# A new order for the 1215 pieces of an attention and feed-forward kernel

## The chip, the cores and the metric

One core of a Trainium2 chip. The metric is the device time of one execution in microseconds (us), lower is better. All engines of the core are used: TensorE (PE) for matmuls, with its weight loads shown apart as PEld, VectorE (DVE), ScalarE (ACT), GpSimd (POOL), SyncE (SP, which only issues DMAs), and the 16 DMA engines.

## The reference

Attention over 4 batches, 8 heads, 768 positions, head size 64, and then a two-layer feed-forward with 512 inputs and 2048 hidden units:

```python
scores = scale * np.matmul(q, k.transpose(0, 1, 3, 2))
stream_keep = causal & (is_sink | in_win)        # 4 sink positions, window of 64
mask = np.where(retr[0, :, 0, 0, None, None], causal, stream_keep)
a = softmax(np.where(mask, scores, -1e9))
x = np.matmul(a, v)                              # heads side by side: 3072 x 512
h = x @ w_in
g = np.maximum(h, 0.0) + alpha * np.minimum(h, 0.0)
out = g @ w_out
```

Heads 0, 2 and 6 are full causal ("retrieval") heads; the other five see only the first 4 positions and the last 64.

## The kernel before

The work is cut into 1215 named pieces. Each piece is a small function that emits a few instructions; `item(name, fn, ...)` stores it, and a list of names, `ORDER`, says in which order all pieces are emitted. The program is scheduled by hand: each engine runs its own instructions in the order in which they were emitted, and waits on semaphores only where a piece needs the result of another engine or a buffer that another engine still uses. So the list is at once the queue of every engine. A piece that waits holds up everything that stands behind it on the same engine, and nothing on the others.

The attention is done in 16 segments n, one for each batch and pair of heads (pairs (2,6), (1,5), (0,4), (3,7)); segments 0 to 3 are the first batch. The names of their pieces:

- `Lq`, `Lk`, `Lv` load rows of q, k and v (lines 234 to 282). They go on SP's queue, q1 in the profile's list of DMA queues.
- `Cq`, `Ck`, `Cv` cast the rows to bf16, on the engine that the strings CQ, CK and CV name for that segment: POOL for segments 1 to 5 (CQ, CK) and 0 to 5 (CV), VectorE for most later ones (lines 351 to 391).
- `Tq`, `Tk` transpose on TensorE (line 406), `tq`, `tk` copy the result out of PSUM (lines 411 to 437). From segment 8 on, `Dq` and `Dk` do this by a transposing DMA on SP.
- `S` computes scores (lines 456 to 473 and 505, 544), `s` exponentiates them on ScalarE (lines 512, 560 to 566), `m` masks them on VectorE (lines 522, 571, 574).
- `A` multiplies with v (line 595), `a` divides by the row sum (lines 605, 606), `X` transposes the result into `xT` (by TensorE, line 620, for segments 0 to 3 and 15, else by DMA on SP, line 614), `x` copies it.

The feed-forward goes by 8 blocks t of tokens, 512 and 256 tokens of each batch in turn:

- `P t.f` multiplies with `w_in` for a group of hidden units (line 640). For some blocks it is cut into parts by input chunk: `P0.f.0` needs segments 0 and 1, `P0.f.1` segment 2, `P0.f.2` segment 3.
- `p` takes the negative part by a relu on ScalarE (line 645), `g` makes the activation on VectorE (line 652).
- Block 0 has its output in pieces `O` (line 660) and `o` (copy, and store on POOL's queue). The other blocks use seven products instead of eight for each 256 x 256 piece (a Strassen-like scheme): `D` are combinations of `w_out`, `Z` those of g (lines 684, 703, VectorE), `Q` the products (line 718), `b1` to `b8` the copies and additions that end in the store (lines 742 to 771).

The weights are loaded on POOL's queue (q0), by a DMA that casts from fp32 to bf16, and so stand in one line with POOL's casts and masks: `wi0a`, `wi0b`, `wi1a`, `wi1b` are half loads for the first 512 hidden units (line 819; the a halves hold the input chunks of segments 0 and 1, the b halves those of 2 and 3), `wi2` to `wi7` the other columns of `w_in` (line 824; 2 and 3 for f 4 to 7, 4 and 5 for f 8 to 11, 6 and 7 for f 12 to 15), `wo0` to `wo3` the rows of `w_out` (line 828). `nr` (line 786) and `ns` (lines 792 to 804) make masks on POOL for the later segments; `kfz` are memsets on POOL. `warm` pieces are matmuls on a buffer of zeros with no reader (line 814).

PSUM has eight banks. `take` gives a piece the bank that was freed longest ago among those that it may use, at the time of emission; so the order also decides which bank a piece waits for.

Scores of segments from 4 on aren't emitted where they stand: `one_score` collects them in `burst`, and `emit_burst` sends the collection when a piece comes that is not in the set of `beside_burst`. Where both heads of a pair have 576 columns or more in the burst, or where the pair is of one kind from segment 8 on, the two heads are sent in turn on the upper and the lower half of the array (64 rows each, line 473), so that they run side by side; else they go one after the other (line 466). So the order also decides how many bursts there are and how they run.

Of the kernel before, what the change touches and what calls it, by code (L numbers as in the profile page):

```python
# [34 lines left out]
A5.0 s7.1.2 O0.3.1 Cv6 m4.1.5 S6.0.2 Cv7 m4.1.3 s7.1.1 Dq8 s6.0.1 O0.3.2 m6.0.4 o0.2 a5.0 m6.0.5 S7.0.0 s7.1.0 Dk9.0
s7.0.2 A6.1 O0.3.3 m6.0.1 S7.0.1 Cq9 m7.1.0 s6.0.2 m6.0.0 s7.0.0 A4.1 m7.0.0 S8.0.0 S8.1.0 s7.0.1 S8.0.5 m6.0.3 S8.1.3
m7.1.1 S8.0.3 a6.1 S8.1.1 m7.1.2 o0.3 s8.0.3 A6.0 X5 a4.1 s8.0.5 A7.1 Q1.0.1 m7.0.2 s8.1.3 s8.1.0 m7.0.1 m6.0.2 s8.1.1
A7.0 a7.1 b1.1.0 Dq9 S9.1.1 a6.0 a7.0 S8.0.2 Lq10 S8.1.4 S8.0.1 X4 Q1.0.2 S9.1.0 S9.0.1 s8.0.0 Z1.0.2 D3.1 S9.0.2
s8.0.1 Z1.0.4 s8.0.2 m8.1.1 S8.1.2 X6 s8.1.4 s9.0.1 Q1.0.5 s8.1.2 Q1.0.6 s9.1.0 s9.0.2 s9.1.1 S8.1.5 D4.0 S8.0.4
S9.0.0 b2.1.0 S9.1.2 X7 s8.1.5 P2.2.0 m8.0.5 P2.11.0 s8.0.4 P2.5.0 m9.1.0 s9.0.0 m8.1.3 m8.0.0 m9.1.1 P2.5.1 Cq10 D3.0  # L40
b3.1.0 P2.2.1 kfz2 s9.1.2 p2.5 m10.0.2 Lk10 m8.0.3 Lv9 p2.2 P2.3.0 P2.3.1 g2.2 nz0 b7.1.0 Q1.0.7 P2.11.1 m9.0.1 g2.5
p2.11 m8.0.4 g2.11 p2.3 P2.1.0 P2.13.0 m8.1.4 b4.1.0 P2.8.0 P2.6.0 P2.1.1 Q1.0.3 P2.8.1 Dq10 m9.1.2 m9.0.2 P2.13.1
m9.0.0 Lq11 P2.7.0 g2.3 p2.1 P2.6.1 p2.13 P2.7.1 Cv9 p2.6 m8.0.1 b8.1.0 P2.9.0 b5.1.0 g2.1 Cq11 g2.6 P2.0.0 P2.15.0
p2.7 g2.7 Ck10 m8.1.0 P2.0.1 p2.8 g2.8 p2.0 P2.14.0 Lv8 A9.0 Lk11 g2.0 Dq11 g2.13 P2.14.1 P2.15.1 P2.4.0 p2.15 P2.4.1
a9.0 p2.14 A9.1 Cv8 Dk10.1 Q1.0.4 g2.14 P2.9.1 b6.1.0 p2.4 P3.0 a9.1 P2.12.0 P2.12.1 P3.4 g2.15 p3.0 A8.0 p2.12
P2.10.0 Dk10.0 P2.10.1 Ck11 S10.1.0 g2.4 Lv11 g2.12 Dk11.0 p2.9 g2.9 Q2.1.1 p2.10 g3.0 b1.2.1 S10.0.1 s10.1.0 p3.4
S10.0.4 s10.0.1 g2.10 Z2.1.1 Q2.0.1 X9 Lv10 b1.2.0 Q2.1.2 S10.0.0 s10.0.0 Z2.0.1 g3.4 Lk14 s10.0.4 S10.0.3 s10.0.3
Z2.1.3 Lk12 a8.0 Q2.0.2 P3.12 b7.2.0 S10.0.5 Lq15 Z2.1.2 b7.2.1 S10.1.2 m10.0.0 S11.0.1 p3.12 S11.1.1 Lq12 Z2.0.3
m14.0.2 m12.0.2 S10.1.1 S11.0.2 Q2.1.6 s11.1.1 s10.1.2 s11.0.2 g3.12 m8.1.5 s10.0.5 b2.2.1 m11.0.2 Z2.0.2 P3.6 s11.0.1
P3.2 b3.2.1 S10.0.2 S11.0.0 S11.1.2 S11.1.0 s10.1.1 s11.0.0 m10.1.2 Q2.1.5 Lv14 A8.1 s10.0.2 m10.1.0 s11.1.0 Q2.1.7  # L50
m10.0.4 m10.0.5 P3.14 m11.1.1 Z2.1.4 p3.6 Cv11 b4.2.1 Q2.0.6 Cv10 m10.1.1 s11.1.2 Q2.1.3 A10.1 g3.6 b5.2.1 Q2.1.4
m10.0.1 m10.0.3 P3.10 b2.2.0 b3.2.0 a8.1 b8.2.1 a10.1 A10.0 kfz3 m11.0.0 m11.1.2 m11.0.1 A11.0 a10.0 p3.2 Q2.0.5
b6.2.1 Lq13 m11.1.0 a11.0 P3.8 A11.1 Q2.0.7 p3.14 X8 Z2.0.4 p3.8 X10 b4.2.0 g3.2 Lk13 Q2.0.3 a11.1 p3.10 Q3.0.1 b8.2.0
b5.2.0 g3.14 P4.12.0 X11 P4.6.0 Lv12 Cq12 P4.1.0 g3.10 g3.8 P4.2.0 Q2.0.4 b1.3.0 P4.5.0 Cq13 P4.12.1 Ck12 P4.6.1 Lv13
P4.15.0 P4.15.1 Z3.0.1 Z3.0.3 P4.1.1 P4.5.1 Lq14 Z3.0.2 p4.12 P4.2.1 g4.12 Dq12 Q3.0.2 p4.2 b7.3.0 Ck13 p4.1 P4.13.0
Ck14 b6.2.0 g4.2 p4.15 Q3.0.6 g4.1 p4.6 p4.5 P4.13.1 g4.15 p4.13 P4.4.0 b2.3.0 Q3.0.5 Dq13 b4.3.0 Z3.0.4 P4.10.0
Dk12.0 P4.8.0 g4.6 P4.14.0 P4.8.1 P4.10.1 b3.3.0 P4.4.1 g4.5 Cv13 Q3.0.7 P4.14.1 P5.2 Q3.0.3 p4.8 g4.8 p4.10 p4.4
b5.3.0 g4.13 g4.4 Lv15 p5.2 P4.3.0 Cv12 p4.14 Cq14 g4.10 P4.3.1 P5.12 S12.0.0 S12.1.2 Cq15 g5.2 p4.3 Dk13.0 Q3.0.4
b8.3.0 g4.14 P5.8 s12.0.0 S12.1.4 p5.12 s12.1.2 S12.0.2 b6.3.0 S12.0.5 S13.1.0 Lk15 P5.6 Dq14 s12.0.5 p5.8 g5.12 p5.6
P4.0.0 P4.11.0 Dk14.1 s12.0.2 g4.3 m12.0.0 Dk14.0 s12.1.4 Cv15 P4.0.1 P4.11.1 s13.1.0 m12.0.5 g5.6 p4.11 P4.7.0 Dq15  # L60
g5.8 P4.7.1 S12.0.1 p4.0 S13.1.2 S12.1.5 g4.11 S13.0.0 P4.9.0 g4.0 s12.0.1 p4.7 P4.9.1 s13.0.0 g4.7 P5.10 P5.4 p4.9
S12.1.0 m12.1.4 S12.1.3 g4.9 S13.0.1 s12.1.5 p5.10 Z4.0.1 S12.0.3 s13.1.2 p5.4 Ck15 s12.1.3 Q4.0.1 g5.4 s12.0.3 g5.10
m13.1.2 Q4.0.5 s13.0.1 s12.1.0 S12.0.4 S12.1.1 S14.1.2 b1.4.0 S13.1.1 m12.0.3 m12.1.3 S14.0.3 Z4.0.3 m12.0.1 S13.0.2
Z4.0.2 m13.1.0 s12.1.1 Q4.0.2 s12.0.4 b7.4.0 Z4.0.4 m12.0.4 s13.1.1 Dk15.0 Q4.1.1 b1.4.1 P5.14 Z4.1.1 A12.0 s13.0.2
s14.0.3 m12.1.5 S14.0.2 m13.1.1 Q4.0.6 m13.0.2 a12.0 S14.0.4 s14.0.2 p5.14 s14.1.2 Z4.1.3 Q4.1.2 b2.4.0 m13.0.0 A13.1
s14.0.4 m14.1.2 S14.0.1 b3.4.0 P5.0 a13.1 b4.4.0 p5.0 Q4.0.3 s14.0.1 Q4.0.7 g5.14 S15.1.2 g5.0 S14.1.1 S14.0.5 S15.0.0
m13.0.1 b5.4.0 m12.1.1 Z4.1.2 S14.0.0 b7.4.1 S15.1.1 m14.0.4 Q4.0.4 s15.1.2 Z4.1.4 s14.0.0 s14.1.1 s14.0.5 m14.0.0
m14.0.1 Cv14 m12.1.0 Q4.1.6 b6.4.0 s15.1.1 m14.0.5 A13.0 b2.4.1 m14.0.3 s15.0.0 S15.0.2 S15.1.0 S15.0.1 S14.1.0
s15.0.2 s14.1.0 m15.0.0 Q4.1.5 s15.1.0 m14.1.1 m14.1.0 A12.1 a13.0 A14.0 s15.0.1 m15.0.2 m15.1.1 a12.1 A14.1 a14.0
Q5.0.1 m15.1.0 a14.1 b3.4.1 b4.4.1 m15.0.1 Q4.1.7 m15.1.2 b1.5.0 X13 X12 b5.4.1 Q5.0.2 Q4.1.3 A15.0 Z5.0.1 X14 a15.0  # L70
A15.1 a15.1 Q4.1.4 b6.4.1 P6.8.0 X15 x15 P6.15.0 P6.4.0 b8.4.0 P6.8.1 P6.11.0 P6.10.0 b8.4.1 b7.5.0 P6.13.0 P6.4.1
P6.2.0 p6.4 P6.10.1 P6.11.1 P6.14.0 P6.2.1 P6.15.1 Z5.0.3 p6.8 p6.11 g6.4 P6.12.0 g6.8 P6.7.0 P6.12.1 P6.7.1 Z5.0.2
p6.15 g6.11 g6.15 P6.3.0 p6.2 g6.2 P6.13.1 p6.10 P6.9.0 P6.14.1 p6.13 P6.3.1 g6.13 p6.7 g6.10 p6.14 P6.1.0 P6.0.0
P6.9.1 g6.14 P6.5.0 p6.9 P6.1.1 p6.12 P6.6.0 g6.7 p6.3 g6.3 P6.6.1 P6.0.1 Q5.0.6 g6.9 P6.5.1 P7.6 p6.1 P7.4 g6.1
# [922 lines left out]
```

## Time and profile before

| | us |
|---|---|
| three runs | 222.61, 223.55, 223.62 (median 223.55) |
| span of the profiled execution, first to last instruction | 220.4 |
| whole time of the profiled execution | not listed apart |
| PE busy | 214.5 |
| DVE busy | 188.0 |
| ACT busy | 145.8 |
| POOL busy | 45.6 |

The median of the runs lies 3.15 us above the span of the profiled execution. In the profile, a "busy" matmul includes a modelled end, which lies behind the start of the next matmul; what TensorE loses is therefore seen better from the distance of the starts. In the rows of the stretches, the numbers are, for PE, PEld, DVE, ACT and POOL in turn, the busy us and in brackets the instructions; then the granted clock, the DMA engines' busy share (which adds up queues that overlap) and GB/s. In rows of the chain and of the timeline the first number is the start and the second the length, both in us.

### The profile page before, as it was taken

Reading aid. Unit: us, or ns where it says so; the run is one execution under the profiler, and the core shown is the slowest. Engines: PE = TensorE matmul, PEld = TensorE weight load, DVE = VectorE, ACT = ScalarE, POOL = GpSimd, SP = SyncE. Lnnn points to the kernel's source line nnn. Section 1 sums busy time; section 2 is a strip of 40 time slices with the busy share of each in tenths; the row PEclk is TensorE's granted clock in tenths of the full one; section 3 lists DMA queues with packets and bytes.
Section 4 is the critical chain, followed back from the end, with each engine's and each line's share of the span. In section 5 each row is a group of like instructions: output and inputs, shape, how many; then the busy total and the mean of one; then the engine's idle time right before and its main releaser. Section 6 shows DMA issues by size and latency. Waiting matters only on the chain.

```text
span 220.4 us, 5779 instructions
## 1 busy us (share of the span) xinstructions
PE 214.5 (97%) x2210; PEld 158.0 (72%) x2210; DVE 188.0 (85%) x471; ACT 145.8 (66%) x314; POOL 45.6 (21%) x92
## 2 busy tenths in 40 slices
...
DMA  6999999999999999979999998791004310002124
GB/s 187 319 233 222 307 241 231 227 201 218 205 245 167 259 162 222 198 182 193 211 215 174 228 184 194 176 187 42 4 1 123 103 79 0 0 3 95 51 93 147
DMA packets 89655, 35.98 MB, mean 163 GB/s; under 512 B 76676, under 2 KB 87964, under 8 KB 89628
## 3 DMA queue, kind: packets, MB, share of 16 engines
...
q10 hardware_dynamic: 320, 0.34, 0.5%
q14 instruction: 10, 0.08, 0.1%
HBM read 27.58 MB, written 6.29 MB: 154 GB/s over the span
## 4 chain that ended last, share of the span: by engine, by line
PE 92%; DVE 3%; ACT 2%; issue 1%
PE P L640 36%; PE P L718 28%; PE P L595 7%; PE P L660 7%; PE P L473 4%; PE P L814 3%; PE P L456 2%; PE P L406 2%; PE P L466 1%; PE P L620 1%; DVE kT L435 1%; PE P L544 1%; DVE g L652 1%; ACT neg L645 1%; ACT kT L435 0%
## 5 line engine op out<-in xcount | busy, mean ns | idle before, releaser
L640 PE MATMUL P<-xT,w_in_b 128*128 128x512 bf16 (+1 forms) x512 | 89.6, 326 | 0.0
L652 DVE SCALAR_TENSOR_TENSOR g<-neg,oma,P 128x256 bf16<-128x256 f32 (+1 forms) x128 | 71.7, 607 | 11.4 <-ACT neg L645 11.0
L645 ACT ACTIVATE neg<-P 128x512 f32<-128x512 f32 x96 | 55.4, 602 | 30.3 <-PE P L640 15.7
L640 PEld LDWEIGHTS <-w_in_b 128*128 128x128 bf16 x512 | 49.2, 98 | 29.1 <-issue 0.3
L718 PEld LDWEIGHTS <-g 128*128 128x128 bf16 x480 | 45.7, 98 | 8.1 <-issue 0.8
L512 ACT ACTIVATE eR<-P 128x448 bf16<-128x448 f32 (+4 forms) x63 | 37.0, 627 | 4.8 <-PE P L505 2.2
L718 PE MATMUL P<-w_out_b,g 128*128 128x256 bf16 x320 | 39.0, 273 | 0.0
...
L560 ACT ACTIVATE eS<-P 128x352 bf16<-128x352 f32 x45 | 20.8, 494 | 2.3 <-PE P L473 1.4
L606 DVE TENSOR_TENSOR xn<-P,rcp 128x448 bf16<-128x448 f32 (+1 forms) x32 | 19.4, 607 | 1.1
L571 DVE TENSOR_TENSOR eS<-eS,ms_near 128x352 bf16<-128x352 bf16 x45 | 15.8, 363 | 0.7 <-ACT eS L560 0.6
L660 PE MATMUL P<-w_out_b,g 128*128 128x512 bf16 x64 | 15.8, 379 | 0.2 <-ACT kT L429 0.2
L703 DVE TENSOR_TENSOR g<-g 128x1024 bf16<-128x1024 bf16 x20 | 13.7, 683 | 0.1
L456 PE MATMUL P<-qT,kT 128*128 128x192 bf16 (+14 forms) x68 | 11.1, 251 | 0.2 <-ACT eS L566 0.2
L595 PEld LDWEIGHTS <-eS 128*128 128x128 bf16 x260 | 10.0, 97 | 1.3
L595 PE MATMUL P<-vb,eS 128*128 128x65 bf16 x260 | 10.8, 193 | 0.0
L522 DVE TENSOR_TENSOR eR<-eR,mr_near 128x128 bf16<-128x128 bf16 (+5 forms) x54 | 10.6, 223 | 0.0
L473 PE MATMUL P<-qT,kT 64*128 64x176 bf16 (+10 forms) x164 | 10.4, 249 | 0.0
L718 PE MATMUL P<-w,g 128*128 128x256 bf16 x80 | 10.4, 273 | 0.0
L660 PEld LDWEIGHTS <-g 128*128 128x128 bf16 x64 | 5.6, 97 | 6.3 <-issue 1.1
L595 PE MATMUL P<-vb,eR 128*128 128x65 bf16 x276 | 10.0, 193 | 0.0
L595 PEld LDWEIGHTS <-eR 128*128 128x128 bf16 x276 | 9.4, 97 | 0.6 <-issue 0.2
(130 smaller groups left out, 267.8 us busy)
## 6 DMA issues: line engine op xcount, KB each, us to landing
out_dram<-ot POOLq DMA_DIRECT2D x18, 256.0 KB, 3.2
...
w_out_b<-in_moe_w_out_dram POOLq DMA_DIRECT2D x4, 512.0 KB, 15.1
...
```

The costliest lines, as they stand in the source:

```text
L456: nc.tensor.matmul(to, keys, queries, start=True, stop=stop)
L473: nc.tensor.matmul(to, keys[own], queries[own], start=True, stop=True)
L512: nc.scalar.activation(ebuf[n, hh][:, lo:hi].rearrange("p (x c) -> p x c", x=len(parts)), P[:, got[0]:got[0] + len(parts), 0:(hi - lo) // ...
L560: nc.scalar.activation(slots, sc[:, 0:352].rearrange("p (s c) -> p s c", c=176), AF.Exp, scale=scale)
L571: nc.vector.tensor_tensor(slots, slots, ms_near[:, 0:2, :] if m == 0 else ms_near[:, 1:3, :], op=ALU.mult)
L595: nc.tensor.matmul(pav[:, i, :], e[:, o:o + 128], vv[:, j, hh, 0:D + 1], start=(m == 0), stop=(m == len(terms) - 1))
L606: nc.vector.tensor_tensor(xn[n][:, 0:nt, D * hh:D * hh + D], pav[:, :, 0:D], rcp.to_broadcast([128, nt, D]), op=ALU.mult)
L640: nc.tensor.matmul(psg[:, w * i:w * (i + 1)], w_in_b[:, c, 128 * fb:128 * (fb + 1)], xT[:, c, o:o + w], start=(x == 0), stop=(x == 3))
L645: nc.scalar.activation(neg[t, f], bank(held["P", t, f][0]), AF.Relu, scale=-1.0)
L652: nc.vector.scalar_tensor_tensor(g_buf[t % 2][:, fb, 0:w], neg[t, f][:, c], oma[:, fb:fb + 1], bank(got[0])[:, c], op0=ALU.mult, op1=ALU.add)
L660: nc.tensor.matmul(bank(held["O", t, s][0]), g_buf[t % 2][:, f, 128 * s:128 * (s + 1)], w_out_b[:, f, :], start=(f == 0), stop=(f == 15))
L718: nc.tensor.matmul(q_bank(t, u, CHAIN[y]), left[t, u][y][:, f, :], right[y][:, f, :], start=(first and f == 0), stop=(f == 7), skip_group_ ...
```

## The change

Only `ORDER` changes. The first 40 names stay where they are, and the other 1175 stand in a new order over the whole rest of the list. No piece is added, removed or changed; each is emitted once. What follows from the list changes with it: the queue of each engine and of its DMAs, the PSUM bank that each piece gets, and the bursts of scores.

In POOL's queue, `wi0a`, `wi1a`, `wi1b`, `wi0b` stood together behind `Ck3.0` and now stand apart, with casts, `nr` and two `kfz` between them; `ns` now stands between `wi2` and `wi3`; `wo1` to `wo3` now stand behind `Cv4`. In SP's queue, `Lq3` now stands ahead of `Lv0`, `Lk4` ahead of `Lv3`, and `Lv4` ahead of `Lk7` and `Lq7`. In TensorE's queue the first pieces of blocks 0 and 1 come in another order, among them `P1.14` and `P0.15` ahead of `P0.13`. The core of the diff: the beginning of both lists, the part of the new one around Cv8, and the ends.

```diff
--- before.py
+++ after.py
 ORDER = """
-busy zero id warm0 kz3 Lq0.0 sz1 vz2 nms nmr so1 vz0 Lq0.1 Lk1 warm8 warm5 warm3 kz1 qz0 one Lq1 Lk0 La Ck0.0 kz2
-Cq0.0 Tq0.0 tq0.0 Tk0.0 qz warm2 Lk2 Lq2 kz0 tk0.0 Ck1.0 Ck1.1 Cq0.1 Tk1 S0.0.1 s0.0.1 Tq0.1 S0.0.0 Cq1 warm7 Lv0
-tk1.0 sz2 vz1 vz3 Tq1 Ck0.1 S0.0.2 s0.0.0 tk1.1 Tk0.1 Ck2.1 tq1 S1.1.0 s0.0.2 Ck2.0 warm4 tq0.1 s1.1.0 Cq2 tk0.1 Cv0
-Lk3 S0.1.0 kfz0 Lv1 vo ro0 Ck3.1 s0.1.0 Lq3 Ck3.0 wi1a wi0a wi1b wi0b Cq3 sz0 idf S1.0.0 so2 Al s1.0.0 so0 al S0.1.1
-s0.1.1 Lv2 Tq2 Tk2 tk2.1 tk2.0 S0.1.2 S1.0.1 A0.0 s0.1.2 a0.0 Cv1 A0.1 a0.1 Cv2 s1.0.1 tq2 S1.1.1 Tk3 S2.0.1 tk3.0
-s1.1.1 S2.0.2 X0 s2.0.1 x0 wi6 s2.0.2 wi7 Lv3 Lq4 Tq3 tk3.1 S2.0.0 wi5 m4.0.2 warm6 S2.1.0 A1.0 a1.0 Lk4 tq3 A1.1
-Cv3.0 s2.0.0 Lq5 Lk6 Lq6 Lk5 wi4 Cq4 a1.1 S3.0.0 s2.1.0 A2.0 s3.0.0 X1 x1 S3.0.1 S3.1.1 Ck4.0 P0.2.0 s3.0.1 A3.0 a2.0
-Lq7 a3.0 S2.1.1 s3.1.1 wi2 s2.1.1 Cv3.1 S3.1.0 wi3 A2.1 Ck4.1 Cq5 wo1 s3.1.0 P0.1.0 P0.3.0 A3.1 Lk7 P0.0.0 Tq4 a2.1
-tq4 X2 a3.1 X3 Lv5 Tk4 x2 P0.2.1 Lv6 P0.1.1 tk4.0 P0.3.1 P0.0.1 x3 Tq5 tq5 tk4.1 P0.0.2 P0.1.2 wo0 p0.0 P0.3.2 P0.13
-p0.13 g0.0 P0.14 g0.13 P1.14 wo3 p0.1 p1.14 g0.1 P1.2 p1.2 P0.8 Lv4 g1.14 Ck6.0 P0.9 g1.2 Cq6 m8.0.2 p0.8 nr p0.9 g0.8
-m12.1.2 p0.3 near0 near2 P0.15 S4.0.5 p0.14 P1.10 s4.0.5 Ck6.1 P0.11 P0.2.2 g0.9 Ck5.1 g0.14 p0.15 p1.10 P1.0 Lq8 Tq6
-ro1 Ck5.0 g0.15 p0.2 g0.3 S4.1.0 g1.10 wo2 p0.11 P1.12 P1.8 P0.7 g0.2 Lk8 s4.1.0 kfz1 g0.11 Lk9 p1.0 P0.5.0 p1.12 tq6
-g1.0 P0.5.1 Tk5 P0.4.0 p1.8 P0.6 tk5.0 g1.8 p0.7 P0.4.1 g1.12 P0.5.2 P0.4.2 p0.6 tk5.1 P0.10 g0.7 p0.4 p0.10 g0.6
-S4.0.3 s4.0.3 S4.0.0 P1.4 g0.4 Tk6 g0.10 S4.0.1 S5.1.0 m4.0.3 P1.6 p0.5 tk6.1 Ck7.0 near1 D1.0 P0.12 tk6.0 O0.0.0 g0.5
-O0.0.1 p1.6 Lv7 p0.12 g1.6 p1.4 S6.1.1 D1.1 s5.1.0 s4.0.0 S5.1.1 S4.1.2 g1.4 m4.1.0 s4.0.1 s4.1.2 Z1.0.1 s6.1.1 s5.1.1
-O0.1.0 S5.0.0 S4.0.4 S4.1.4 S4.1.1 g0.12 O0.1.1 s5.0.0 m4.0.5 s4.1.4 m4.0.0 Ck7.1 s4.1.1 ns S5.1.2 S4.0.2 S4.1.3
-S5.0.1 O0.0.2 s5.1.2 s4.1.3 D2.1 O0.0.3 O0.2.0 s5.0.1 m6.1.1 S6.0.4 s4.0.4 S5.0.2 S6.1.0 D4.1 m5.0.0 s4.0.2 Z1.0.3
-S6.0.0 m5.1.2 o0.0 S6.1.2 S4.1.5 Lq9 Cq7 Cv4 s5.0.2 m5.1.1 O0.1.2 D2.0 Tk7 s4.1.5 O0.2.1 Cv5 Tq7 m4.0.1 m5.0.2 s6.1.0
-m8.1.2 s6.1.2 O0.1.3 tk7.0 m5.1.0 m4.0.4 tk7.1 A4.0 Ck8 s6.0.0 tq7 A5.1 m4.1.2 S6.0.5 o0.1 m4.1.1 O0.2.2 Cq8 Dk8.0
...
-Q6.1.6 Z6.0.4 Q6.0.3 g7.12 b7.6.0 b8.6.0 b2.6.1 Q6.0.7 Z7.0.1 Z7.0.3 b3.6.1 b5.6.0 Q6.1.5 Q7.0.5 b4.6.1 Q6.0.4 Z6.1.4
-b1.7.0 Z7.0.2 Q7.0.2 Q6.1.7 Q7.0.6 Q6.1.3 b5.6.1 b4.7.0 b2.7.0 b7.6.1 b7.7.0 b6.6.0 b8.6.1 b3.7.0 Q6.1.4 Q7.0.7 b6.6.1
-Z7.0.4 Q7.0.3 b5.7.0 Q7.0.4 b8.7.0 b6.7.0
+busy zero id warm0 kz3 Lq0.0 sz1 vz2 nms nmr so1 vz0 Lq0.1 Lk1 warm8 warm5 warm3 kz1 qz0 one Lq1 Lk0 La Ck0.0 kz2 Cq0.0
+Tq0.0 tq0.0 Tk0.0 qz warm2 Lk2 Lq2 kz0 tk0.0 Ck1.0 Ck1.1 Cq0.1 Tk1 S0.0.1 S0.0.0 Lq3 s0.0.1 warm4 Cq1 s0.0.0 vz1 tk1.1
+Tq1 S0.0.2 Tq0.1 Ck0.1 tk1.0 Ck2.0 tq1 Cq2 Lv0 Lk3 Ck2.1 Cq3 s0.0.2 Tk0.1 warm6 tq0.1 S1.1.0 tk0.1 idf S1.0.0 s1.1.0
+warm7 S0.1.0 vz3 Cv0 sz2 Tq2 s1.0.0 S0.1.1 vo s0.1.0 Tk2 Al wi0a Ck3.0 S0.1.2 s0.1.1 s0.1.2 sz0 Ck3.1 al Lv1 so0 wi1a
+Lv2 A0.0 S1.0.1 tq2 s1.0.1 Cv1 nr tk2.1 ro0 A0.1 kfz3 S1.1.1 kfz1 Lk4 Tk3 tk2.0 ro1 Lv3 a0.1 a0.0 Cv2 tk3.0 s1.1.1
+S2.0.1 S2.0.0 s2.0.1 A1.0 a1.0 A1.1 Ck4.1 s2.0.0 S2.0.2 a1.1 Tq3 wi1b X0 s2.0.2 S2.1.0 tq3 wi6 tk3.1 X1 Ck4.0 S3.0.0 x0
+s2.1.0 Cv3.0 S3.0.1 A2.0 Lq4 Lq5 s3.0.0 s3.0.1 x1 S2.1.1 Cq4 s2.1.1 so2 S3.1.0 a2.0 A2.1 Cv3.1 Lq6 Tq4 S3.1.1 s3.1.0
+wi0b a2.1 A3.0 s3.1.1 Tk4 wi7 Cq5 P0.3.0 wi2 X2 tk4.0 ns Cq6 a3.0 wi3 wi4 A3.1 a3.1 tq4 P0.1.0 x2 P0.0.0 P0.2.0 wi5 Lk5
+Tq5 P0.3.1 P0.0.1 near0 P0.1.1 X3 Lk6 Tq6 P0.2.1 tq5 x3 P1.14 near2 S4.0.5 P0.2.2 Lv4 tq6 P0.0.2 P0.15 tk4.1 p0.2 P0.1.2
+s4.0.5 g0.2 P1.2 p0.0 P0.3.2 p1.14 g0.0 Lk7 Ck5.0 p1.2 g1.14 g1.2 p0.15 p0.1 g0.15 g0.1 Ck5.1 S4.1.4 P1.0 p0.3 wo0 P0.14
+Tk5 p0.14 S4.1.0 P1.4 g0.3 P0.13 Ck6.0 s4.1.0 Cv4 P0.9 p1.0 g0.14 p1.4 kfz0 tk5.1 g1.0 S4.0.3 Ck6.1 tk5.0 g1.4 P0.8 p0.9
+S5.1.2 P1.6 Lk8 s4.0.3 near1 g0.9 Lq8 P1.8 P0.5.0 p0.13 g0.13 p0.8 Lq9 P1.12 S4.0.0 s5.1.2 g0.8 D1.0 p1.6 P0.4.0 p1.8
+s4.1.4 m4.0.5 P0.11 s4.0.0 Tk6 P0.6 g1.6 p0.11 g1.8 P0.4.1 P0.5.1 p1.12 Ck7.0 p0.6 wo1 g0.11 S5.1.0 P0.7 wo2 g0.6 P0.5.2
+S5.1.1 g1.12 tk6.1 P0.4.2 P1.10 p0.7 s5.1.0 m5.1.2 s5.1.1 g0.7 p1.10 p0.5 Lv6 P0.12 Ck8 wo3 g0.5 tk6.0 p0.4 P0.10 m5.1.0
+S4.0.1 s4.0.1 O0.1.0 p0.12 O0.0.0 S5.0.0 g1.10 S5.0.2 g0.4 p0.10 g0.12 S6.1.2 S6.1.0 Lq7 O0.1.1 Lv5 O0.0.1 s6.1.2 s6.1.0
+Lk9 Z1.0.1 S6.1.1 s5.0.2 S4.1.3 S4.1.5 S4.0.4 g0.10 s5.0.0 S4.0.2 S5.0.1 s4.1.3 m4.0.1 Ck7.1 Cv5 D2.0 m4.0.0 m4.0.3
+O0.0.2 S6.0.4 s4.0.4 s4.0.2 m5.0.0 m5.0.2 s5.0.1 O0.0.3 S6.0.0 s6.1.1 S6.0.5 S4.1.2 s4.1.5 S4.1.1 m4.0.4 m4.1.5 Cq8
+s4.1.1 o0.0 O0.1.2 m5.0.1 m6.1.2 A4.0 s6.0.5 s6.0.0 Lv7 m5.1.1 s6.0.4 s4.1.2 m6.0.5 Tk7 m4.1.3 Cv6 kfz2 m6.1.0 m6.0.4
+O0.1.3 m6.1.1 S6.0.1 O0.2.0 O0.3.0 Cq7 S6.0.2 O0.2.1 Tq7 s6.0.1 O0.2.2 m6.0.1 tk7.0 Dk8.0 tq7 A5.0 o0.1 Ck9 a4.0 O0.2.3
+m4.1.0 s6.0.2 Z1.0.3 m4.1.1 S6.0.3 tk7.1 S7.0.1 Cq9 s7.0.1 m4.1.4 O0.3.1 a5.0 m7.0.1 D1.1 Dq8 o0.2 A5.1 s6.0.3 S7.0.2
...
+P2.12.1 g2.2 p2.15 P2.10.1 g2.1 Ck11 m8.0.1 g2.15 P2.4.1 P2.9.0 A9.1 Lq11 P2.13.0 Q1.0.4 Cq11 P2.0.1 p2.12 a9.1 Dk10.0
+p2.10 P2.13.1 g2.10 p2.4 g2.12 P2.9.1 p2.0 g2.4 P2.8.0 p2.9 S10.0.0 Lv8 P2.14.0 g2.0 P2.8.1 b6.1.0 Dq11 A9.0 Dk11.0
+p2.13 Dk10.1 Cv8 m8.1.4 p2.8 g2.13 a9.0 A8.0 g2.9 m8.0.2 P2.14.1 S10.0.4 P3.0 P3.4 Q2.0.1 a8.0 Lv10 g2.8 S10.0.1 S10.0.3
+s10.0.4 p2.14 S11.1.2 p3.0 s10.0.0 g3.0 S11.1.0 Lv11 Q2.1.1 p3.4 s10.0.1 P3.14 s11.1.0 s11.1.2 g2.14 b1.2.0 m8.1.0 g3.4
...
+g7.8 b1.6.1 Z6.1.2 Z6.0.2 p7.10 Q6.0.2 Q7.0.1 Q6.1.6 Q6.0.6 Z6.0.4 g7.10 b2.6.1 Z7.0.1 b2.6.0 b4.6.0 Q6.0.3 Q6.1.2
+b3.6.0 Q7.0.5 Z7.0.3 Q6.0.7 b3.6.1 Z7.0.2 b5.6.0 b7.6.0 Q7.0.6 b1.7.0 Q6.0.4 Z6.1.4 Q6.1.7 b4.6.1 b8.6.0 b2.7.0 Q7.0.2
+b3.7.0 b4.7.0 b6.6.0 b7.7.0 Q6.1.3 b5.6.1 b7.6.1 Q7.0.7 Q6.1.4 Z7.0.4 b5.7.0 Q7.0.4 b8.6.1 b6.6.1 b6.7.0 Q7.0.3 b8.7.0
 """.split()
```

81 lines of the change are left out of this document (37 added, 44 removed).

## The prediction

> **What bounds the kernel now.** I read the page first, then the busy time by stretches of 10 us, the waits of TensorE, the chain, and last the timeline of POOL with the landing of its loads.
>
> ```profile
> span 220.4 us, 5779 instructions
> PE 214.5 (97%) x2210; PEld 158.0 (72%) x2210; DVE 188.0 (85%) x471; ACT 145.8 (66%) x314; POOL 45.6 (21%) x92
> DMA  6999999999999999979999998791004310002124
> PE 92%; DVE 3%; ACT 2%; issue 1%
> ```
>
> TensorE holds 92% of the chain and is busy 97% of the span. The DMA row says something else as well: the 16 engines are full for the first 25 slices of 5.5 us. So TensorE sets the time, and for the first 130 us or so the loads leave little room.
>
> ```profile
> 0.00:10.00 10.00, 8.94 (x109) 8.31 (x110) 6.86 (x21) 5.99 (x7) 6.29 (x19) 1.00 0.81 253
> 10.00:20.00 10.00, 9.05 (x146) 7.85 (x144) 8.46 (x25) 8.59 (x12) 8.37 (x15) 1.00 1.12 232
> 50.00:60.00 10.00, 9.80 (x66) 4.66 (x65) 9.46 (x28) 9.78 (x25) 0.00 (x0) 1.00 1.10 210
> ```
>
> TensorE's first number shows where time could still be won: it is 8.94 and 9.05 of 10 in the first two stretches, 9.80 in 50 to 60, and 10.00 in nearly all others. A reordering cannot win much after 20 us. It can lose anywhere.
>
> ```profile
> PE P L778 <- DVE ident_f L324: 0.4, 1, 0.4
> PE P L406 <- DVE kT L437: 0.4, 1, 0.4
> PE P L660 <- ACT kT L429: 0.2, 1, 0.2
> 51.11 0.80 ACT kT L429
> 51.95 1.24 PE P L660 x5
> ```
>
> Of TensorE's waits, the two of 0.4 us fall at 13.8 and 10.5 us, behind the place where the lists part (about 8 us). The only one after 20 us is the third: the first output piece (O0.0.0, line 660) starts at 51.95, when ScalarE's copy at 51.11 frees a PSUM bank. Counted from the matmul starts just before it, 0.4 us are lost (0.20 shown idle, the rest inside a modelled end).
>
> **Part 1, TensorE's own work.** No matmul is added, but scores that stand together in the list are sent as one burst, and the two heads' bursts run side by side on half arrays.
>
> ```profile
> 131.29 0.86 PE P L640 x4
> 138.45 1.74 PE P L640 x12
> 140.19 0.30 PE P L473 x2
> 140.49 0.98 PE P L718 x8
> 142.83 3.57 PE P L640 x20
> ```
>
> Four 512-column matmuls take 0.86 us, so 215 ns each, and 448 columns are worth 0.19. The burst of two 448-column scores side by side takes 0.30, and the eight 256-column products behind it take 0.98 where eight of them are worth 8 x 0.108 = 0.87. Going in and out thus costs 0.11 + 0.11, about 0.2 us a burst. By the rule in lines 477 to 505 I counted the side-by-side bursts off both lists: 17 before, 21 after. Four more cost 0.8 us; the columns that must stream through them come out 0.08 us shorter. **+0.7 us**, certain in sign.
>
> **Part 2, the weights of the first layer.** POOL's queue is one line: casts, masks and weight loads run in the order of the list. The loads wi0a to wi7 move back in it.
>
> ```profile
> 11.02 0.83 POOL L351 CAST g<-rows 128x768 bf16<-128x768 f32 x1 [0.17 <-DMA rows<-in_q_dram]
> 12.75 0.93 POOL L391 CAST vb<-rows 128x896 bf16<-128x896 f32 x1 [0.90 <-DMA rows<-in_v_dram]
> 13.62 0.23 POOL L324 MEMSET rows<- 128x128 f32 x1
> 14.35 0.95 POOL L364 CAST g<-rows 128x384 bf16<-128x384 f32 x2 [0.50 <-DMA rows<-in_k_dram]
> 15.24 2.55 POOL L819 DMA_DIRECT2D w_in_b<-in_moe_w_in_dram  x4
> 19.55 0.63 POOL L342 COPY vb<-vb 4x192 f32<-4x192 f32 x2
> 20.14 0.92 POOL L391 CAST vb<-rows 128x896 bf16<-128x896 f32 x1
> 21.42 1.85 POOL L824 DMA_DIRECT2D w_in_b<-in_moe_w_in_dram  x3
> 23.72 0.56 POOL L386 CAST vb<-rows 128x448 bf16<-128x448 f32 x1 [0.45 <-DVE xn L606]
> 24.34 0.34 POOL L342 COPY vb<-vb 4x192 f32<-4x192 f32 x1
> 31.58 1.28 POOL L786 TENSOR_SCALAR_AFFINE_SELECT mr_near<-one 128x1248 bf16<-128x1248 bf16 x1
> 42.16 0.34 POOL L792 TENSOR_SCALAR_AFFINE_SELECT ms_near<-one 128x176 bf16<-128x176 bf16 x1
> 45.28 0.32 POOL L804 COPY ms_near<-ms_near 128x176 bf16<-128x176 bf16 x1
> ```
>
> Before, all four half loads go out from 15.24 on. In the new list POOL has done the same casts up to the end of Cq2 (11.02 + 0.83 = 11.85). From there to wi1b it runs Cq3 0.83, Cv0 0.93, wi0a 0.62, Ck3 2 x 0.5, wi1a 0.62, Cv1 0.93 + 0.63, nr 1.28 (line 786, moved up from 31.58), two kfz 0.46, Cv2 0.92 + 0.34, Ck4.1 0.5: 9.1 us, and with about 1 us for rows that are not there yet (0.90 and 0.50 before) wi1b issues at 22.0. Behind it come wi6, Ck4.0, Cv3.0 (0.56 + 0.34), Cq4, so **wi0b issues at 25.5**; wi7 26.1, Cq5, wi2 27.6, then ns, which took 42.16 to 45.60, 3.44 us, and so wi3 31.6, wi4 32.3, **wi5 32.9**.
>
> ```profile
> L819 POOL DMA_DIRECT2D w_in_b<-in_moe_w_in_dram x4: 606/615/774, 15.2 to 17.2; - x4
> DMA to landing us min/median/max: 4.6/6.4/7.4
> L824 POOL DMA_DIRECT2D w_in_b<-in_moe_w_in_dram x6: 608/620/641, 21.4 to 27.0; - x6
> DMA to landing us min/median/max: 7.0/10.5/11.9
> q0 software_dynamic: 3650, 3.58, 81.2%
> q1 hardware_dynamic: 3717, 2.16, 37.6%
> w_in_b<-in_moe_w_in_dram POOLq DMA_DIRECT2D x6, 256.0 KB, 10.5
> ```
>
> The two lines of queues are for 26 to 52 us: q0, POOL's, moved 3.58 MB in 26 us, 0.138 MB/us, beside q1, SyncE's rows. A 256 KB load needs 1.9 us at that rate, a half 0.95. The least time to landing, less the transfer, is 3.7 us for a half load and 5.1 for a whole one. So wi1b lands at 26.6 to 28.1, middle 27.3; then in a row wi6 29.2, **wi0b 30.2, wi7 32.1**, wi2 34.0. wi3 is issued late and cannot profit from the queue: 31.6 + 5.6 to 7.0 = 37.2 to 38.6, then wi4 39.8, **wi5 41.7**.
>
> ```profile
> 30.00 0.95 PE P L640 x4
> ```
>
> TensorE began the second parts of the first hidden pieces (P0.2.1) at 30.00, behind 24.50 us of matmuls in its list. The new list has 24.45 us in front of P0.3.1, the first that reads wi0b: 29.9. I add no gain before it; the early idle time may shrink or grow by 1 us. P0.3.1 waits 0.3 us for wi0b. P1.14 stands 1.6 us of matmuls behind it and needs wi7: 31.8 against 32.1, again 0.3. P0.9 stands 7.8 us further (seven hidden pieces of 0.87, four thirds of 0.215, one transposition, three scores) and needs wi5: 39.9 against 41.7, **1.8 us**. Together +2.4, from 0 (fastest start, wi3 queued without a gap) to 3.1. Everything behind P0.9 on TensorE waits with it, and ScalarE's relu and VectorE's product behind that. No cover is left: PSUM holds eight banks, and the next P0.8 needs the same weights.
>
> **Part 3, the weights of the second layer.** wo1 to wo3 now stand behind Cv4 on POOL, which waits for the rows of Lv4.
>
> ```profile
> 40.35 0.95 POOL L364 CAST natk<-rows 128x384 bf16<-128x384 f32 x2 [7.49 <-DMA rows<-in_k_dram]
> ```
>
> Before, the 18th load of rows (Lk5) ended a wait of 7.49 us at 40.35. Lv4 is the 19th in the new list. One load of 0.39 MB more at q1's 2.16 MB in 26 us is 4.7 us; but q0 lies empty longer before 25 us, which gives about that back. Taken between: Lv4 at 43, wo3 issued at 45.5, three loads of 0.52 MB at 0.138: 44 + 3.7 + 11.4 = 59.1. O0.0.3 needs it at about 60, counted from P0.9. I take +0.2 us, 0 to 1.
>
> **Part 4, what goes.** ScalarE, busy 9.78 of 10 in the stretch from 50 to 60, has 12.7 us of pieces beside the 12 us of matmuls from the 40th on in the list before, and 9.8 in the new one; so the wait at 51.95 goes: -0.4. What is late next there is the weights. The later rows and transposes I cost at nothing. Their cover is the matmuls between a piece's place and its first reader: at least 5.1 us from attention's result to the layer in both lists, at least 3.8 us from a cast of queries or keys to its scores before and 6.4 in the new list. Thin is one place: Cv8 stands right before A8.0, which reads it, where the list before has 3.7 us between; should TensorE be held up there by that cast's own length, it costs some 0.6 us, and that is in the range. The end changes from a copy on ScalarE to an addition on VectorE: 0.05.
>
> **Sum.** 0.7 + 2.4 + 0.2 - 0.4 = +2.9 us on the span of 220.4. The profiled execution's whole time is not listed; the median of the runs, 223.55, lies 3.15 above the span, and I carry that over: **226.4 us**.
>
> **Rivals.** *The weights are in time.* If each load lands as the fastest did, 4.6 us after issue, wi0b is there at 30.1, wi7 at 30.7 and wi5 at 37.5, before P0.9 at 39.9. Then only +0.7 - 0.4 stay: 223.9. For it: q0 was idle before 25 us, so its loads start with nothing ahead. Against it: the whole loads took at least 7.0 and 10.5 in the median. [...]
>
> *The second layer's weights set the time.* If Lv4 lands at 47 instead of 43 (one load of rows at the shared rate further back), wo3 lands at 63.1 and O0.0.3 waits 3 us more: 229.4. It decides from the point where Lv4 lands later than 44. For it: q1's share falls to 37.6% whenever POOL's queue is full. Against it: rows get more while POOL's queue starts late.
>
> *Faster: attention's start is the gain.* The waits of 0.4 and 0.4 us behind the parting of the lists are 1.6 us when the gaps are counted from start to start, with a third at 12.5. If the new order of the first scores fills them, and POOL comes 2 us earlier because no row is waited for, so that no weight is late, the sum is -1.6 - 0.4 + 0.7 = -1.3: 222.2. It decides when wi5 goes out before 31. Against it stands POOL's plain sum of work: 12.6 us lie ahead of wi0b.
>
> **Chances.** Forecast 0.55 (own range 224.9 to 228), weights in time 0.18, second layer late 0.15, attention faster 0.12. About 0.5%, 1.1 us, is what a measurement of this kernel can tell from no change. Faster by that 0.12, within it 0.17, slower 0.71. The range cuts off the ends of the outer rivals: **222.8 to 229.8**.
>
> **What would show it.** TensorE's wait in front of line 640 for the landing of w_in, first near 30 us and largest near 40; POOL's ns before wi3, with wi5 issued near 33; none at 51.95; 21 bursts with the same 0.2; the rest of TensorE at 10.00 of 10. I am wrong if line 640 never stands still between 29 and 43, if the loss lies behind 90 us, where VectorE is nearly full, or if the first 20 us differ by more than 1.

## The result, and the profile after

The new list takes 228.62 us (median of four runs, 227.79 to 228.98) where the list before takes 223.21 on the same chip (222.61 to 223.62): 1.024 times as long (95% interval 1.020 to 1.027), 5.4 us more. The forecast was 226.4, in a range to 229.8. The profiled execution took 228.27 us with a span of 226.6. So 1.67 us lie outside the span, not the 3.15 that I carried over; the profiled execution of before must have been one of its shorter ones. Executions more than 1.5% above the fastest of their kernel (two of run 1's four, one of run 9's seven) are left out of the medians and ratios below.

The page of the new kernel, the lines that answer to those of before:

```profile
span 226.6 us, 5795 instructions
PE 216.6 (96%) x2210; PEld 157.8 (70%) x2210; DVE 187.0 (83%) x471; ACT 145.3 (64%) x314; POOL 45.8 (20%) x92
PE 62%; issue 18%; DMA 13%; POOL 3%; DVE 2%; SPq 1%; ACT 0%; POOLq 0%; DVEq 0%; ACTq 0%
```

TensorE is busy for 2.1 us more and the span is 6.2 us longer, so most of the loss is waiting; and the chain, which was TensorE for 92%, now has 13% of DMA ("issue" is time for which the profile shows no wait). The stretches of the new kernel (first number after the length: PE's busy us) say where:

```profile
0.00:10.00 10.00, 8.20 (x95) 7.55 (x96) 5.83 (x19) 4.96 (x6) 6.30 (x19) 1.00 0.77 251
10.00:20.00 10.00, 9.86 (x166) 8.60 (x164) 8.30 (x24) 9.19 (x14) 7.40 (x13) 1.00 1.00 220
20.00:30.00 10.00, 9.01 (x169) 8.29 (x166) 7.28 (x21) 7.20 (x11) 9.19 (x17) 1.00 1.13 285
30.00:40.00 10.00, 7.71 (x65) 5.25 (x64) 4.14 (x12) 6.29 (x11) 6.16 (x18) 1.00 1.21 212
40.00:50.00 10.00, 9.48 (x70) 6.14 (x68) 9.66 (x23) 9.41 (x23) 3.23 (x5) 1.00 1.22 208
50.00:60.00 10.00, 10.00 (x68) 5.35 (x66) 8.88 (x20) 8.70 (x21) 0.00 (x0) 1.00 1.01 186
100.00:110.00 10.00, 9.48 (x107) 6.71 (x105) 9.93 (x22) 7.70 (x18) 0.72 (x1) 1.00 1.04 202
```

The first 20 us hold as much work as before (8.20 + 9.86 against 8.94 + 9.05). The wait of before between 50 and 60 is gone. The holes are between 20 and 50 us, and a smaller one behind 100. TensorE's waits name them:

```profile
PE P L638 <- DMA w_in_b<-in_moe_w_in_dram: 2.3, 1, 2.3
PE P L404 <- POOL natq L349: 1.0, 1, 1.0
PE P L638 <- DVE g L650: 0.5, 1, 0.5
PE P L593 <- DVE vb L389: 0.4, 1, 0.4
```

The largest is P0.3.1 in front of line 638 (line numbers are two less than before): the reader was forecast, but with 0.3 us, and the largest wait at P0.9. The second, Tq4 behind the cast of its queries, was not forecast. (natq and natk are the casts of queries and keys, vb those of v.) The chain from 27 us on, and POOL's timeline:

```profile
27.07 6.68 DMA w_in_b<-in_moe_w_in_dram
...
33.88 0.81 PE P L638 x3
...
42.85 0.56 DVE natk L362
43.41 0.66 DVE g L650
...
44.09 1.02 PE P L638 x4
```

```profile
14.93 0.94 POOL L389 CAST vb<-rows 128x896 bf16<-128x896 f32 x1 [1.55 <-DMA rows<-in_v_dram]
23.18 0.50 POOL L362 CAST natk<-rows 128x384 bf16<-128x384 f32 x1 [0.67 <-DMA rows<-in_k_dram]
...
26.25 0.87 POOL L349 CAST natq<-rows 128x768 bf16<-128x768 f32 x1
27.07 0.59 POOL L817 DMA_DIRECT2D w_in_b<-in_moe_w_in_dram  x1
33.05 1.83 POOL L822 DMA_DIRECT2D w_in_b<-in_moe_w_in_dram  x3
39.99 0.94 POOL L389 CAST vb<-rows 128x896 bf16<-128x896 f32 x1 [3.45 <-DMA rows<-in_v_dram]
```

wi0b goes out at 27.07 instead of the 25.5 of the forecast, and lands at 33.75 instead of 30.2. The last three w_in loads go out from 33.05 on, 1.5 us later than forecast. Cv4 is there at 39.99, earlier than the 43 that I took, and w_out holds nothing up.

### The profile page after: what moved, and what is told of

Read it like the earlier page. It is cut to its first block, busy times and chain, and to the rows that moved or that the text cites. A ratio compares the mean times of both kernels' runs of the same rounds, so it can differ in the third digit from the quotient of the medians.

```text
span 226.6 us, 5795 instructions
## 1 busy us (share of the span) xinstructions
PE 216.6 (96%) x2210; PEld 157.8 (70%) x2210; DVE 187.0 (83%) x471; ACT 145.3 (64%) x314; POOL 45.8 (20%) x92
## 4 chain that ended last, share of the span: by engine, by line
PE 62%; issue 18%; DMA 13%; POOL 3%; DVE 2%; SPq 1%; ACT 0%; POOLq 0%; DVEq 0%; ACTq 0%
PE P L638 25%; PE P L716 20%; PE P L658 6%; DMA rows<-in_k_dram 5%; PE P L471 4%; PE P L593 4%; DMA rows<-in_v_dram 3%; DMA w_in_b<-in_moe_w_in_dram 3%; DMA out_dram<-ot 2%; DVE g L650 2%; PE P L464 1%; PE P L404 1%; POOL w_in_b L817 1%; POOL out_dram L734 1%; POOL vb L389 0%
## 5 line engine op out<-in xcount | busy, mean ns | idle before, releaser
L638 PE MATMUL P<-xT,w_in_b 128*128 128x256 bf16 (+1 forms) x512 | 90.9, 326 | 3.0 <-DMA w_in_b<-in_moe_w_in_dram 2.3
L638 PEld LDWEIGHTS <-w_in_b 128*128 128x128 bf16 x512 | 49.0, 98 | 32.3 <-issue 4.8
L716 PEld LDWEIGHTS <-g 128*128 128x128 bf16 x480 | 45.7, 98 | 9.1 <-DVE g L701 0.8
L716 PE MATMUL P<-w_out_b,g 128*128 128x256 bf16 x320 | 40.6, 273 | 0.1
L734 POOL DMA_DIRECT2D out_dram<-ot x14 | 8.1, 579 | 119.9 <-DVE ot L769 41.8
L558 ACT ACTIVATE eS<-P 128x352 bf16<-128x352 f32 x45 | 19.8, 484 | 0.6 <-PE P L471 0.6
L569 DVE TENSOR_TENSOR eS<-eS,ms_near 128x352 bf16<-128x352 bf16 x45 | 14.2, 332 | 0.8 <-ACT eS L558 0.8
L471 PE MATMUL P<-qT,kT 64*128 64x176 bf16 (+12 forms) x168 | 11.5, 250 | 0.0
L746 ACT COPY rows<-P 128x256 f32<-128x256 f32 x9 | 3.3, 378 | 11.6 <-DVE P L743 11.5
L389 POOL CAST vb<-rows 128x896 bf16<-128x896 f32 x5 | 4.7, 934 | 27.9 <-PE P L404 22.9
## 6 DMA issues: line engine op xcount, KB each, us to landing
w_out_b<-in_moe_w_out_dram POOLq DMA_DIRECT2D x4, 512.0 KB, 11.9
```

Of the source, the lines that this page charges most:

```text
L471: nc.tensor.matmul(to, keys[own], queries[own], start=True, stop=True)
L558: nc.scalar.activation(slots, sc[:, 0:352].rearrange("p (s c) -> p s c", c=176), AF.Exp, scale=scale)
L569: nc.vector.tensor_tensor(slots, slots, ms_near[:, 0:2, :] if m == 0 else ms_near[:, 1:3, :], op=ALU.mult)
L638: nc.tensor.matmul(psg[:, w * i:w * (i + 1)], w_in_b[:, c, 128 * fb:128 * (fb + 1)], xT[:, c, o:o + w], start=(x == 0), stop=(x == 3))
L716: nc.tensor.matmul(q_bank(t, u, CHAIN[y]), left[t, u][y][:, f, :], right[y][:, f, :], start=(first and f == 0), stop=(f == 7), skip_group_ ...
```

## The experiments

The theory was that the w_in loads stand too late in POOL's queue; the rival that the rest of the order costs the time. All kernels differ from one of the two in `ORDER` alone, but for the last. The list before was timed again beside each group, and the ratios go by that: 222.67 us beside runs 1 to 4, 222.91 beside 5 to 7, 223.03 beside 8 to 10, 222.15 beside 11. PE 10-60 is TensorE's busy time in the 50 us from 10 to 60 of the one profiled execution.

| run | us | times before (95%) | PE 10-60 |
|---|---|---|---|
| before | 223.21 | 1 | 48.85 |
| new list | 228.62 | 1.024 (1.020 to 1.027) | 46.06 |
| 1 weights late in the old list | 230.40 | 1.035 (1.031 to 1.040) | 42.45 |
| 2 weights early in the new list | 229.34 | 1.031 (1.027 to 1.035) | 44.71 |
| 3 new first part | 227.64 | 1.022 (1.019 to 1.025) | 44.19 |
| 4 new second part | 225.35 | 1.012 (1.009 to 1.015) | 48.05 |
| 5 two half loads early | 229.11 | 1.027 (1.024 to 1.031) | 45.73 |
| 6 weights and one row load early | 230.96 | 1.036 (1.033 to 1.038) | 43.89 |
| 7 one row load early | 229.59 | 1.031 (1.029 to 1.034) | 45.93 |
| 8 rows read later | 227.63 | 1.021 (1.015 to 1.027) | 46.90 |
| 9 one row load read earlier, old list | 228.31 | 1.024 (1.020 to 1.029) | 43.32 |
| 10 run 8, and Cv8 earlier | 228.64 | 1.023 (1.017 to 1.028) | 45.86 |
| 11 run 2 with fewer bytes | 225.21 | 1.011 (1.005 to 1.017) | 47.35 |

**Run 1: the weights late in the old list.**

```diff
-Ck3.0 wi1a wi0a wi1b wi0b Cq3
+Ck3.0 wi1a wi0a Cq3
...
-Cv1 A0.1 a0.1 Cv2
+Cv1 nr A0.1 a0.1 Cv2 wi1b wi6
...
-wi4 Cq4
+Cq4 wi0b wi7
...
-Cq5
+Cq5 wi2 ns wi3 wi4 wi5
```

> The list of before with nothing moved but the weights of the first layer and the two masks on POOL: nr behind Cv1, wi1b and wi6 behind Cv2, wi0b and wi7 behind Cq4, then wi2, ns, wi3, wi4, wi5 behind Cq5, as the new list has them beside the casts. Theory (late loads on POOL carry the larger half of the loss): P0.3.1, the first reader of wi0b, waits about 1.5 to 2.5 us near 30 us, P0.9 up to 1.8 near 40, and the time is 2.5 to 4 us above before, 226 to 227. Rival (the loss is spread over the rest of the order: first scores, bursts, VectorE): within 0.8 us of before.

The trace, and PE 10-60 in the table, are of a further execution of the same kernel, 232.03 us.

> The first run's kernel once more for its trace. Theory: a wait for w_in of 3 us or more, longer than in the new list because the list of before reads wi5 sooner, and the granted clock at half for about 3 us behind it, as behind the stalls of 3.05 and 4.0 us in the second and third run; together about 7 us, as its time says. Rival: no single wait above 2.5 us and the clock at 1.0 throughout; the 7 us lie in many places.

```profile
PE P L639 <- DMA w_in_b<-in_moe_w_in_dram: 6.5, 3, 4.7
```

Late loads by themselves cost 7.8 us (6.8 to 8.8), far more than forecast, because the old list reads wi5 sooner: three readers wait 6.5 us, one of them 4.7. From within that wait on the granted clock stood at half for 6.8 us (the last section has what this costs). So the place of the loads in POOL's queue can be the whole price of a list. The rival is out for this kernel.

**Run 2: the weights early in the new list.** Weights and masks go back to the casts behind which the old list has them.

```diff
-wi0a Ck3.0
-Cv1 nr
-Tq3 wi1b X0
-wi0b a2.1
-Tk4 wi7 Cq5
...
+Ck3.1 wi1a wi0a wi1b wi0b
+Cv2 wi6 wi7 wi5
+Cv3.0 wi4
+Cq4 wi2 wi3
+Cq5 wo1 wo0 wo3 nr
+Ck5.1 wo2 ns
```

> The new list with the weights and masks alone put back to where the list of before has them beside POOL's casts. Theory: the wait in front of line 638 for w_in goes, and the time falls 2.5 to 4 us below the new kernel, to about 225; what is left above before is bursts and small waits. Rival: within 0.8 us of the new kernel, because the 2.3 us at P0.3.1 only hides another wait that then shows.

The theory fails here. The wait for w_in is gone, and others stand in its place. TensorE's waits of this run, VectorE's, and the chain:

```profile
PE P L465 <- DVE g L651: 2.9, 1, 2.9
PE P L405 <- POOL natq L350: 1.5, 1, 1.5
```

```profile
DVE natk L363 <- DMA rows<-in_k_dram: 4.1, 1, 4.1
```

```profile
23.41 30.39 DMA rows<-in_k_dram x2
```

The chain's row covers two loads. The cast is Ck7.0, of keys on VectorE, and it waits until 53.8 for the first half of Lk7, which SP's queue reaches at 35.74; in the new list it is reached at 29.91. SP's timeline of this run, and that of the new list:

```profile
35.74 7.28 SPq L253 DMA_DIRECT2D rows<-in_k_dram  x2
```

```profile
29.91 5.62 SPq L252 DMA_DIRECT2D rows<-in_k_dram  x2
```

The activations g stand behind the cast, hold their PSUM banks, and TensorE stops at 51.7. So rows are late now where weights are early, those of `w_out` too, which came forward with `w_in` in this run.

**Runs 3 and 4: one part of each list.** The cut is at Q1.0.1 of the new list and at Q1.0.7 of the old one, where PSUM has banks free for the other list to go on. The edit is written short here.

```diff
-ORDER = OLD
+ORDER = NEW[:k] + [x for x in OLD if x not in NEW[:k]]
...
-ORDER = OLD
+ORDER = OLD[:k] + [x for x in NEW if x not in OLD[:k]]
```

> The new list up to its piece Q1.0.1 (about 66 us of TensorE's work), behind it the remaining pieces in the order of the list of before; 19 side-by-side bursts instead of 21. Theory (the loss lies before 45 us): 4 to 5 us above before, about 227.5. Rival (the loss lies in the later stretches): no more than 2 us above before.

> The list of before up to its piece Q1.0.7 (about 75 us), behind it the remaining pieces in the new order; 20 side-by-side bursts. Theory: 1 to 2 us above before, about 224.8, most of it between 100 and 135 us with a wait of A8.0 for the cast Cv8 of 0.4 to 0.6 us. Rival: 4 us or more above before.

The first part costs 5.0 us and the second 2.7. The theory holds for the first; the second is above the 1 to 2 expected. They add up to more than the 5.4 of both together: each has its own seam, and the bursts are 19 and 20 as counted off the lists, so two and three more than before.

Run 3 also shows how far one trace can be trusted. Up to the cut its list is the new one, name for name, and P0.3.1 waits 3.9 us where it waited 2.3:

```profile
PE P L638 <- DMA w_in_b<-in_moe_w_in_dram: 3.9, 1, 3.9
```

So a difference of 1.6 us in one wait between two traces need not come from the list. In the second part, TensorE's holes lie where VectorE and ScalarE feed it (first number after the length):

```profile
80.00:90.00 10.00, 9.37 (x68) 5.49 (x65) 7.24 (x23) 7.01 (x20) 0.00 (x0) 1.00 1.23 193
90.00:100.00 10.00, 9.76 (x64) 5.19 (x62) 9.97 (x21) 5.31 (x10) 0.59 (x1) 1.00 0.97 185
```

That is 0.9 us. Three bursts of 0.2 make 0.6, and 0.8 lie in 10 to 60 us, where this list is the old one; these are a difference between two executions and no price of the second part.

**Runs 5, 6 and 7: smaller moves.** Run 5 takes two half loads forward in the new list; run 6 takes Lk6 forward in run 2's; run 7 takes Lk6 alone forward in the new list.

```diff
-Tq3 wi1b X0
-wi0b a2.1
+wi1a wi1b wi0b
...
-X3 Lk6 Tq6
+Lq5 Lk6 s3.0.0
```

> The new list with two half loads moved alone: wi1b and wi0b directly behind wi1a, so that wi0b goes out near 18.5 instead of 27.07. Theory (POOL's queue as a whole is late, not one load): the 2.3 us in front of P0.3.1 go, and the readers behind it wait instead, P1.14 about 1.5 to 2.5 us for wi7 and P0.9 about 1 to 2 us for wi5; time within 1.5 us of the new kernel, about 227.5. Rival (this one load is the loss): 2.3 us or more below the new kernel, 226 or less, with no other wait for w_in.

> The kernel with the weights back at their places (the second run), and beside that Lk6 moved ahead of Lq6 and Lk5, as the list of before has it. Theory (weights and rows share one stream of about 0.22 MB/us; with the weights early, Lk6 comes two loads too late and stops VectorE at 53.8): the stall of 3.05 us at 51.7 and the 3 us at half clock behind it go, and the time falls from 229.3 to about 225. Rival (the early issues themselves hold POOL's casts up): 228 or more.

> The new list with Lk6 alone moved ahead of Lq6 and Lk5; the weights stay late. Theory: P0.3.1 still waits 2 to 3 us for wi0b, P0.9 still waits for wi5 (it landed at 43.95), so within 1 us of the new kernel, 227.6 to 229.6. Rival (the rows are the cause, the weights only show it): 2 us or more below the new kernel.

From run 5 TensorE's waits and a row of POOL's timeline, from run 6 the same and a row of the chain:

```profile
PE P L404 <- POOL natq L349: 2.0, 1, 2.0
PE P L593 <- DVE kT L435: 0.9, 1, 0.9
PE P L638 <- DMA w_in_b<-in_moe_w_in_dram: 0.5, 1, 0.5
```

```profile
26.55 0.72 POOL L384 CAST vb<-rows 128x448 bf16<-128x448 f32 x1 [2.05 <-DMA rows<-in_v_dram]
```

```profile
PE P L405 <- POOL natq L350: 3.3, 1, 3.3
PE P L405 <- ACT qT L410: 2.1, 1, 2.1
```

```profile
27.15 0.72 POOL L385 CAST vb<-rows 128x448 bf16<-128x448 f32 x1 [2.72 <-DMA rows<-in_v_dram]
```

```profile
24.39 12.82 DMA rows<-in_q_dram
```

In run 5 P0.3.1 no longer waits, and P1.14 waits 0.5 us for wi7, less than expected; but Tq4 waits 2.0 instead of 1.0, and a product with v that had not waited waits 0.9: no gain. Tq4's wait begins on POOL, where Cv3.0 stands ahead of Cq4 and waits 2.05 us for rows of v.

Run 6 was a miss, 231 instead of 225, and its expectation names the wrong load: what stopped VectorE in run 2 was Lk7, and Lk6 had been there in time. With Lk6 forward Lq6 is pushed back (12.82 us to landing). Its cast holds ScalarE up, and Tq6 waits 2.1 behind it; Tq4 waits 3.3, because Cv3.0 waits 2.72. VectorE no longer stops, but TensorE also comes there later by these waits.

Run 7 came as expected; P0.3.1 waits 3.0 us. In these three lists nothing that was brought forward won time, and in runs 5 and 6 what waits instead waits for rows. I count weights and rows as one stream, for in two different orders they moved together at nearly the same rate, 235 and 225 GB/s; here the DMA totals of before and of run 2 between 18 and 54 us:

```profile
DMA packets 12111, 8.47 MB, mean 235 GB/s; under 512 B 4693, under 2 KB 12105, under 8 KB 12105
```

```profile
DMA packets 12085, 8.12 MB, mean 225 GB/s; under 512 B 4947, under 2 KB 12079, under 8 KB 12079
```

So I formed another theory: what counts is how many bytes must be there before a given matmul. Counted off the lists (0.393 MB for a load of rows, 0.131 for a half load of w_in, 0.262 for a whole one), the old list needs 6.98 MB for P1.14 and what stands ahead of it, the new one 7.37, because Tq6 has moved ahead of P1.14 and brings Lq6 with it. At the first reader of wi5 it is 7.50 against 8.81, though that reader stands some 4 us of matmuls later.

**Run 8: the readers of rows later.** The w_in loads early, and Tq4, Tk4, Tk5, Tq6 with their loads and casts further back among the first layer's pieces.

```diff
-Cv3.1 Lq6 Tq4 S3.1.1
-s3.1.1 Tk4 wi7 Cq5
-X3 Lk6 Tq6 P0.2.1
-P0.14 Tk5 p0.14
...
+Lq5 Lk5 Lq6 Lk6 s3.0.0
+P0.0.0 Tq4 P0.2.0 Tk4 Tq5 tq4
+P0.9 Tk5 p1.0
+P0.8 Cq6 p0.9
+P1.8 Ck6.0 Tq6 P0.5.0 Ck6.1
```

> The new list with the w_in loads and masks early again, and besides that the readers of three loads of rows moved later among the first layer's pieces: Tq4 and Tk4 behind P0.0.0 and P0.2.0, Tk5 behind P0.9 and Tq6 behind P1.8, with their loads (Lk5, Lq6, Lk6, in that order) and casts (Cq6, Ck6) to match. Theory (what counts is how many bytes must have come in before a given matmul, at about 0.225 MB/us for weights and rows together; the new list asks for 7.37 MB before P1.14 where the list of before asks for 6.98, and for 8.81 instead of 7.50 before the reader of wi5): no wait above 1.5 us between 20 and 60 us, and about 225, that is before plus 0.7 for bursts and 1.4 behind 100 us. Rival (the early issues hold POOL up, whatever is read when): 228 or more, as in the second, fifth and sixth run.

```profile
PE P L639 <- DVE g L651: 0.8, 1, 0.8
```

Half a success. The trace is of the fastest of the four executions, 226.38 us. In it no wait after the start is above 0.8 us, as expected, and TensorE is busy 46.90 us of the 50; but many small waits are left, and the median is 227.6 instead of 225. Its interval overlaps that of the new list, so a gain of 1 us is not shown.

**Run 9: one load of rows read earlier, in the old list.**

```diff
-Lq5 Lk6 Lq6 Lk5
+Lq5 Lq6 Lk6 Lk5
...
-g1.2 Cq6 m8.0.2
-Lq8 Tq6 ro1
+Cq5 Cq6 wo1
+P0.0.1 Tq6 x3
```

> The list of before with one load of rows used earlier: Lq6 ahead of Lk6, Cq6 behind Cq5, Tq6 behind P0.0.1 instead of P1.0 (10 us of matmuls earlier), tq6 behind P0.0.2; nothing else. Theory (bytes before a reader): 0.39 MB more are needed before P1.14, so 1 to 2 us slower than before, in waits of TensorE for w_in or for rows between 24 and 45 us. Rival (a transposition moved under cover costs nothing): within 0.5 us of before.

The trace is of the longest of the seven executions, 231.78 us, so its waits are at the upper end. TensorE's and ScalarE's longest wait, and the chain:

```profile
PE P L594 <- ACT eS L565: 5.8, 1, 5.8
```

```profile
ACT natq L350 <- DMA rows<-in_q_dram: 5.6, 1, 5.6
```

```profile
20.62 11.90 DMA rows<-in_q_dram
...
32.59 0.83 ACT natq L350
33.42 0.72 ACT eS L565
```

The rival (covered, so free) is out: 5.4 us (4.3 to 6.4). But the price is not that of the bytes, 1 to 2 us, either. Lq6 lands 11.9 us after its issue; ScalarE stands in the cast Cq6 for 5.6 us, and the exponentials behind it wait though their scores are ready. This read, too early, was paid at the landing of its own load, and by everything behind the cast on its engine.

**Run 10: Cv8 earlier,** in run 8's list.

```diff
-S10.0.0 Lv8 P2.14.0
-Dk10.1 Cv8 m8.1.4
+Lv9 Lv8 m9.0.0
+Cv9 Cv8 P2.2.0
```

> The kernel of the eighth run with one thing more: the load Lv8 directly behind Lv9 and the cast Cv8 directly behind Cv9, some 8 us of matmuls ahead of A8.0 instead of directly before it. Theory: the wait of 0.6 us in front of A8.0 near 103 us goes, and the time is 0.3 to 0.6 us below the eighth run. Rival (VectorE is full there and the wait only moves to another piece): within 0.2 us of the eighth run.

TensorE's busy time from 100 to 140 us, run 8 and run 10:

```profile
100.00:140.00 40.00, 39.88 (x417) 30.39 (x416) 38.91 (x96) 21.62 (x52) 3.19 (x5) 1.00 0.99 194
```

```profile
100.00:140.00 40.00, 39.46 (x409) 29.60 (x407) 38.91 (x95) 20.80 (x50) 3.03 (x5) 1.00 0.93 180
```

Nothing is won. VectorE is busy 38.9 of 40 us in both, and the waits stand at other pieces. Run 8's execution had no wait at A8.0 to take away, so this says little on Cv8 itself.

**Run 11: run 2's list with fewer bytes.**

```diff
+        if 4 <= n < 7:
+            eng.dma_start(flat[:, 0:6 * D], dram(q, first, [[6 * D, 128], [1, 6 * D]]))
+            return
...
+            if 4 <= n < 7 and hh:
+                continue
```

> The kernel of the second run (weights early, 229.34 us, 3.1 % above before) in its unchanged order; only, the loads of queries and keys of the segments 4, 5 and 6 bring the first head's rows alone, and the second head computes on old rows. That takes six times 0.197 MB, 1.18 MB, out of the stream before 40 us; no other instruction changes. Theory (bytes before a reader): 1.18 MB at 0.225 MB/us are 5.2 us, as much as TensorE stood idle there between 10 and 60 us (5.3), so the stall of 3.05 us near 52 and the 1.5 us for Tq4 go and the time is 224 to 225.5, 0.5 to 1.3 % above before. Rival (POOL's and the other engines' order is the cause, the rows come in time): 228 or more, 2.5 % or more above before.

```profile
10.00:60.00 50.00, 47.35 (x536) 34.02 (x533) 40.15 (x101) 41.32 (x78) 26.06 (x50) 1.00 1.14 218
```

As the bytes have it: 225.21. With 1.18 MB out of the stream, the 3.05 us stall and half of Tq4's wait (0.8 instead of 1.5) are gone with no piece moved; the time falls from 1.031 to 1.011 times before. Lk7 is whole in this run, but SP's queue reaches it at 25.40 where it was 35.74:

```profile
25.40 7.23 SPq L258 DMA_DIRECT2D rows<-in_k_dram  x2
```

It shows that the loads of rows ahead of it (their bytes, and three DMAs that fall away with them), not the order on POOL, held run 2's list up. For the new list itself, whose weights are late, it was not tried.

## Why the prediction was right or wrong

The sign came as forecast, and so did the stretch that holds the larger part of the loss, 20 to 50 us. The size did not: +2.9 us on the span against +6.2, and the constant outside the span, wrong the other way, hid 1.5 us of that. Without it the range would have ended at 228.3 and the measured 228.62 would lie outside; that part was luck. From start to start of TensorE's matmuls, in the one trace (the bursts' 0.7 is the price of one, read off it, times four):

| step | forecast | measured |
|---|---|---|
| P0.3.1 for wi0b | 0.3 | 2.45 |
| P1.14 for wi7 | 0.3 | 0 |
| P0.9 for wi5 | 1.8 | 0.7 |
| Tq4 for its queries | 0 | 1.16 |
| four bursts | 0.7 | 0.7 |
| w_out | 0.2 | 0 |
| the wait at 51.95 | -0.4 | -0.4 |
| A8.0 behind Cv8 | 0, up to 0.6 | 0.6 |
| other small waits from 100 to 135 us | 0 | 0.8 |

*Part 1* was right: 21 bursts, each with 0.1 us in and 0.1 out. No run isolates it.

The largest shortfalls are 1.4 us behind 100 us, 1.16 at Tq4 and 0.75 at the three readers of w_in.

*Part 2* had the mechanism and not the size. Behind Cq2, from where the forecast counts, POOL waited 2.2 us for rows ahead of wi0b (1.55 and 0.67) where I allowed "about 1 us", and Cq2 itself 0.98 where it had been 0.17. The half load then took 6.68 us where I took 4.7. The three readers lost 3.15 us together against 2.4, most of it at the first: that wait of 2.3 us gave the later loads time, and P1.14 lost nothing behind it. P0.9's wait has two causes within 0.15 us, wi5 (34.25 + 9.70 = 43.95) and the cast natk on VectorE in the chain; they can't be told apart.

*Part 3*: Lv4 came 3 us earlier than I took, and the rival that rests on it fell.

*Part 4* holds the step that failed: "The later rows and transposes I cost at nothing. Their cover is the matmuls between a piece's place and its first reader." Tq4 cost 1.16 us. The cover was counted from a cast to its scores; but the cast's first reader is the transposition, and the cast stands in the queue of POOL that Part 2 makes late. By Part 2's own sum Cq4 ends at 25.5; it ended at 27.07, having started without a wait of its own, directly behind Cv3.0. (By the trace's semaphores its rows landed at about 26.2, just as POOL came to it, so the queue and the load can't be told apart.) That a load read too early has a price of its own, run 9 shows with 5.4 us.

Why no reordering of the loads won the time back is shown in part. In run 2's list the demand for bytes is the cause (run 11); in runs 5 and 6 waits for rows took the place of those for weights. That the same demand holds the new list up, so that POOL's queue sets where TensorE waits and the demand sets that it waits, is argued from the counted megabytes and was not tested on that list.

*Rivals*: weights in time, and attention's start as a gain, both fell; the first 20 us hold as much work as before. A part of the loss does lie behind 80 us: 1.4 us in the trace, of which the range allowed for A8.0's 0.6 and I had put the rest at 0, and 2.7 us for run 4's list.

Open stay the small waits of run 8 between 18 and 47 us, and the 2.7 us of run 4: 0.9 and 0.6 of it have a place in the second part, 0.8 is a difference between two executions.
